# Mask factors copied by GpSimd, earlier turns, other PSUM banks and split last stores in an attention and Fourier-mixing kernel

## The chip, the cores and the metric

The kernel runs on one core of a Trainium2 chip. The metric is the time of one execution on the device, in microseconds (us), as the median of several runs. Besides it there is one profiled execution, whose span, from the first to the last instruction, is about 1 us shorter than the time of a run.

The core has five engines that the text names: TensorE (PE in the profile, its weight loads PEld) multiplies matrices into PSUM; VectorE (DVE), ScalarE (ACT) and GpSimd (POOL) work element by element; SyncE (SP) issues DMA transfers. They run side by side and wait for each other by semaphores. SBUF is the memory on the chip, HBM the one beside it.

## What is computed

Attention with a block mask over 4 batches of 8 heads, then a Fourier mixing and a two-layer network over each batch, all in float32:

```python
# bigbird attention: q, k, v are (4, 8, 768, 64), blocks of 32
scores = q @ k.T / sqrt(64)
# kept: neighbouring blocks, first and last block row and column, 3 sampled blocks a row
attn = softmax(where(mask, scores, -1e9)) @ v
x = attn.transpose(0, 2, 1, 3).reshape(4, 768, 512)
# fnet mixing: w_ch1 is (512, 2048), w_ch2 is (2048, 512)
u = x + real(fft(fft(x, axis=1), axis=2))
un = (u - mean(u)) / sqrt(var(u) + 1e-6)
out = u + maximum(un @ w_ch1, 0) @ w_ch2
```

## The kernel before

The program handles heads two at a time: a *pair* is two heads of one batch, numbered 0 to 15, four for each batch. A pair has 12 *units*: two halves of the queries (384 each), each against six chunks of 128 keys. A *slot* is two units, so a pair has 6 slots. *Phase* p is the four pairs of batch p; from phase 1 on, the mixing and the network of the batch before run beside the attention. Which instruction comes next on each engine is settled while the program is built, by a model of the engines' times (`when`, `busy`, `gap`).

The mask comes in two ways. Where it is made by TensorE, two bfloat16 factors are multiplied into the scores' PSUM bank, which adds a large negative number to the masked ones. The factors lie in buffers that later hold sums (`acc`), so near the end of phase 0 they are copied elsewhere, into a buffer (`big2`) that has held a chunk of the network's weights:

```python
def keep_factors():                                   # called in slot 19 of 24 of phase 0
    kept = room(2, [P, 2, S], "factors", BF16)        # the buffer "big2"
    for a, t in enumerate(factors["at"]):             # at_k and at_q, 128 x 768 each
        nc.sync.dma_start(out=kept[:, a, :], in_=t)
    factors["at"] = kept[:, 0, :], kept[:, 1, :]
...
def w_round(i):            # one of 32 chunks: rounds the weights, ScalarE and then VectorE
    ...
    nc.vector.tensor_add(out=dst, in0=dst, in1=a.bitcast(FP32))      # L462
...
def scores(us):            # for two units
    ...
    nc.tensor.matmul(s[:, i, 0:HS], kT[rows, c * P:(c + 1) * P], qT[rows, queries], ...)      # L570
    ...
    nc.tensor.matmul(s[:, i, 0:HS], at_k[rows, ...], at_q[rows, queries], ...)                # L580
def weigh(u, s):           # exponentials, one of four buffers "e"
    nc.scalar.activation(out=e, in_=s[:, :, 0:HS], func=ACT.Exp, scale=scale)                 # L590
def gather(u):             # sums the six e of a half into "acc", from pair 4 on
    ...
    nc.vector.tensor_tensor(out=acc, in0=start, in1=e, op=ALU.add)                            # L614
    # or, where the model has VectorE busy:
    for i in range(2):
        nc.gpsimd.tensor_add(out=acc[:, i, :], in0=start[:, i, :], in1=e[:, i, :])            # L619
def values(u):             # products of e with v                                             # L633
def total(n):              # row sums of a pair from its two acc, by TensorE                  # L715
```

From pair 5 on, q and k come into the kernel's layout (*turns*) not by TensorE but by these three steps for each pair:

```python
def squares(n, a):         # ScalarE, only for a check on the largest score                   # L527
def flip_blocks(n, a):     # VectorE transposes blocks of 32 x 32: q in place, k into kT
    nc.vector.transpose(out=out, in_=t)                                                       # L537
def in_order(n):           # ScalarE copies q into qT                                         # L545
```

The mixing folds x into sums and differences (VectorE, `fold_0` to `fold_2`, L766 to L794), multiplies along the sequence (`along`, four steps g) and across it (`across`). PSUM has two banks "m", one bank "t" and others. The step g = 2 uses two:

```python
ps = ps_m.tile([P, 512], FP32, tag="m", name="zp")
...
if g == 2:
    side = ps_m.tile([P, 512], FP32, tag="m", name="side")
    at = bank("m")
    ...
...
nc.scalar.copy(out=zs[:, g - 2, 0:KS - 1], in_=ps[:, 0:KS - 1])                               # L845
...
def un_flip(half, m):      # transposes the normalized rows by TensorE
    tag, pool = (("t", ps_t), ("m", ps_m))[half]
def channels(r, half, m):  # products of the network, bank "m"                                # L1089
```

The order within a slot, cut to what matters here:

```python
def slot(sl):
    ...                                  # values of an earlier slot, scores
    for u, ps in got:
        weigh(u, ps)
    if not paired and not late:
        gap(1.5)                         # steps of the mixing, here the folds
    ...
    if BY_VECTOR <= n + 1 < len(pairs):  # turns of the next pair
        for at, fn, args in ((0, squares, (n + 1, 0)), (1, flip_blocks, (n + 1, 0)),
                             (2, in_order, (n + 1,)), (4, flip_blocks, (n + 1, 1)),
                             (5, squares, (n + 1, 1))):
            if s == at:
                fn(*args)
```

The last batch's network uses a scheme with seven block products for each of three output tiles m, and stores two tiles of 128 rows for each m (xA: tile m, xB: tile m + 3). Tile 5, the last of xB, is one transfer of two runs of 64 rows; tile 2, the last of xA, is two transfers of 64 rows.

```python
# outputs(r, m, after): a0, a1 and b0, b1 are the left and right halves of xA and xB
...
plus(b1, p5)
ahead(2)                                               # operands of the next m
plus(b0, product(ps_s, "s", a22, rights[4]))           # sixth product
if r == 1:
    store(1, m)                                        # xB
ahead(3)
p3 = product(ps_m, "m", o_s[m, 4], block(r, 1, 1))     # seventh product
plus(a1, p3)
if r == 1:
    store(0, m)                                        # xA
ahead(4)
```

Of the kernel before, what the change touches and what calls it, by code (L numbers as in the profile page):

```python
# [102 lines left out]
def kernel(  # L103
# [14 lines left out]
    nc = tc.nc  # L118
# [77 lines left out]
    def bank(tag):  # L196

        at = free[tag].index(min(free[tag]))
        when["PE"] = max(when["PE"], free[tag][at])
        free[tag][at] = float("inf")  # L200
        return tag, at
# [273 lines left out]
    def keep_factors():  # L475

        kept = room(2, [P, 2, S], "factors", BF16)
        for a, t in enumerate(factors["at"]):
            nc.sync.dma_start(out=kept[:, a, :], in_=t)
        factors["at"] = kept[:, 0, :], kept[:, 1, :]  # L480

    turned, e_of, acc_of, o_of, sums_of, x_of, sp_of = {}, {}, {}, {}, {}, {}, {}
# [272 lines left out]
    def fourier(b, xA, xB, uns):  # L755
# [45 lines left out]
        def along(g):  # L801

            sa, sd, e1 = st["f"]
            if g == 0:
                st["zc"] = zc_p.tile([P, 2, KS], FP32, tag="zc", name="zc")
            ps = ps_m.tile([P, 512], FP32, tag="m", name="zp")
            odd = S // 4

            def cosine(ps, rows, cols):
                mm = nc.tensor.matmul
                for t in (0, 2):
                    mm(ps[rows, 0:KS], sa[:, t, cols], cs_sb[:, t, :], start=(t == 0), stop=False)  # L814
                mm(ps[rows, 0:odd], e1[:, cols], cs_sb[:, 1, 0:odd], start=False, stop=False)
                mm(ps[rows, odd:KS], sa[:, 1, cols], cs_sb[:, 1, odd:KS], start=False, stop=True)

            def keep_cosine(dst, ps):
                nc.scalar.copy(out=dst, in_=ps[:, 0:KS])

                nc.scalar.copy(out=_grid(dst, P + 1, 2, 63, 63, 1),
                               in_=_grid(ps, P, 2, 65, 63, 1))
                nc.scalar.copy(out=_run(dst, P, 2, P - 1), in_=_run(ps, P + 64, 2, -1))

            if g < 2:
                cosine(ps, slice(0, P), parts[g])
                keep_cosine(st["zc"][:, g, :], ps)
                return
            if g == 2:
                side = ps_m.tile([P, 512], FP32, tag="m", name="side")  # L830
                at = bank("m")
                for i, (lhs, t, cols) in enumerate(((sa[:, 0, :], 0, slice(0, KS)),
                                                    (sa[:, 2, :], 2, slice(0, KS)),
                                                    (e1, 1, slice(0, odd)),
                                                    (sa[:, 1, :], 1, slice(odd, KS)))):
                    g32 = 32 * min(i, 2)
                    nc.tensor.matmul(side[g32:g32 + 32, cols], lhs[:, QD:QD + 32],
                                     cs_sb[:, t, cols], start=True, stop=True,
                                     tile_position=(0, g32))
                st["zs"] = room(0, [P, 3, KS], "zs")  # L840
            zs = st["zs"]
            for t in range(T):
                nc.tensor.matmul(ps[:, 0:KS - 1], sd[:, t, parts[g - 2]], sn_sb[:, t, :],  # L843
                                 start=(t == 0), stop=(t == T - 1))
            nc.scalar.copy(out=zs[:, g - 2, 0:KS - 1], in_=ps[:, 0:KS - 1])  # L845
            if g == 2:
                keep_cosine(zs[0:96, 2, :], side[0:96, :])
                give(at, busy("PE", 0.8) + 1.5)
# [72 lines left out]
        def d(us, fn, *args):  # L921
# [4 lines left out]

        first = [d(1.8, fold_0, 0), d(1.8, fold_0, 1), d(1.0, fold_1, 0), d(0.9, fold_e),
                 d(1.0, fold_1, 1), d(1.2, fold_2, 0), d(0.6, fold_2, 2), d(1.3, fold_2, 1)]
        first += [("M" if g == 2 else "m", lambda g=g: along(g), 2.1, (1.0 if g < 2 else 0.5), 0.0)
                  for g in range(4)]  # L930
        pq = [("m", lambda m=m: across(m), 2.6 if m == 1 else 1.6, 0.7, 0.95) for m in range(T)]
        ar = [[d(1.4 if m == 1 and half == 1 else 1.0, arrive, half, m) for m in range(T)]
# [11 lines left out]
    def mixer(b, xA, xB):  # L944
# [6 lines left out]
        def un_flip(half, m):  # L951
            if half not in unT:
                unT[half] = tr_p.tile([P, ND, T * P], FP32, tag="tr", name="unT")
            un = uns.pop((half, m))
            tag, pool = (("t", ps_t), ("m", ps_m))[half]
            tp = pool.tile([P, ND, P], FP32, tag=tag, name="utp")
            for d in range(ND):
                nc.tensor.transpose(tp[:, d, :], un[:, d * P:(d + 1) * P], ident)  # L958
            nc.scalar.copy(out=unT[half][:, :, m * P:(m + 1) * P], in_=tp)
# [134 lines left out]
            if r == NF // 4 - 1:  # L1094
                store(half, m)

        def store(half, m):
            x = (xA, xB)[half]
            for p0, cnt, rows in _rows(out[b], T * half + m):
                nc.sync.dma_start(out=rows, in_=x[p0:p0 + cnt, m, :])  # L1100
            if m == T - 1:
                finished.add((b, half))

# [34 lines left out]
        def outputs(r, m, after):  # L1138

            if m == 0:  # L1140
                output_left(m, 1)
                output_left(m, 2)
            a11, a12, a21, a22 = (hs[g, i][:, :, m * P:(m + 1) * P]
                                  for i in range(2) for g in range(2))
            a0, a1 = xA[:, m, 0:DH], xA[:, m, DH:DM]
            b0, b1 = xB[:, m, 0:DH], xB[:, m, DH:DM]
            rights = {j: [o_t[j, 0], o_t[j, 1]] for j in (1, 2, 3, 4)}

            def product(pool, tag, a, c):
                ps = pool.tile([P, 512], FP32, tag=tag, name="yy")[:, 0:DH]  # L1150
                for k in range(4):
                    nc.tensor.matmul(ps, a[:, k, :],  # L1152
                                     c[k // 2][:, k % 2, :] if isinstance(c, list) else c[:, k, :],
                                     start=(k == 0), stop=(k == 3))
                busy("PE", 1.75)
                return ps

            def plus(to, a, c=None):
                tt(out=to, in0=a, in1=to if c is None else c, op=ALU.add)
                busy("DVE", 0.43)  # L1160

            def ahead(j):
                if after is not None:
                    output_left(after, j)

            u = sum_p.tile([P, DH], FP32, tag="oT", name="u")
            p1 = product(ps_m, "m", a11, block(r, 0, 0))
            nc.scalar.copy(out=u, in_=p1)
            plus(a0, p1)
            plus(a0, product(ps_m, "m", a12, block(r, 1, 0)))  # L1170
            if m == 0:
                output_left(m, 3)
                output_left(m, 4)
            plus(u, product(ps_t, "t", a21, rights[2]), u)
            plus(a1, u)
            p5 = product(ps_o, "o", o_s[m, 1], rights[1])
            plus(a1, p5)
            ahead(1)
            plus(u, product(ps_s, "s", o_s[m, 3], rights[3]), u)
            both = xB[:, m, :].rearrange("p (n d) -> p n d", n=2)  # L1180
            tt(out=both, in0=both,
               in1=u.rearrange("p (o d) -> p o d", o=1).broadcast_to([P, 2, DH]), op=ALU.add)
            busy("DVE", 0.7)
            plus(b1, p5)
            ahead(2)
            plus(b0, product(ps_s, "s", a22, rights[4]))
            if r == 1:
                store(1, m)
            ahead(3)
            p3 = product(ps_m, "m", o_s[m, 4], block(r, 1, 1))  # L1190
            plus(a1, p3)
            if r == 1:
                store(0, m)
            ahead(4)

        fl = [[("tm"[h], lambda h=h, m=m: un_flip(h, m), 0.6, 0.55, 0.0) for m in range(T)]
              for h in range(2)]

        before = first + [pq[0], ar[0][0], ar[1][0], sp[0][0],
# [44 lines left out]
    def do_apart():  # L1244
# [5 lines left out]
            return  # L1250
        done = state["ready"]
        if kind != "-":
            at = bank(kind.lower())
            done = busy("PE", pe, done) + HOP
        fn()
        if act:
# [7 lines left out]
    def gap(rest=0.0, ahead=None, kinds="tm"):  # L1264
# [4 lines left out]
        while apart:  # L1269
# [7 lines left out]
                if max(when["DVE"], state["ready"]) + dve > when["PE"] + rest + ahead:  # L1277
                    break
            elif kind != "-":
                bank_at = (max if kind == "M" else min)(free[kind.lower()])  # L1280
                if kind.lower() in used or max(state["ready"], bank_at) > when["PE"] + 0.1:
                    break
                used += kind.lower()
            do_apart()
        for item in list(short):
            kind, ready, fn = item
# [48 lines left out]
    def slot(sl):  # L1335
# [25 lines left out]
            sum_up()  # L1361
        for u, ps in got:
            weigh(u, ps)
        if not paired and not late:
            gap(1.5)
        while due and (opens or not paired):
# [70 lines left out]
        while short and (not more or soon) and (  # L1437
# [4 lines left out]
            item = ready[0] if ready else short[0]  # L1442
            short.remove(item)
            item[2]()
        if BY_VECTOR <= n + 1 < len(pairs):
            for at, fn, args in ((0, squares, (n + 1, 0)), (1, flip_blocks, (n + 1, 0)),
                                 (2, in_order, (n + 1,)), (4, flip_blocks, (n + 1, 1)),
                                 (5, squares, (n + 1, 1))):
                if s == at:
                    fn(*args)  # L1450
        w_loads()
        w_steps(sl)
        if sl == SB - 5:
# [143 lines left out]
```

## Time and profile before

| | us |
|---|---|
| time, median of 3 runs (1080.32 to 1081.24) | 1080.54 |
| span of the profiled execution | 1079.5 |
| TensorE busy | 1042.1 (97%) |
| VectorE busy | 661.5 (61%) |
| ScalarE busy | 376.4 (35%) |
| GpSimd busy | 227.4 (21%) |
| mean granted TensorE clock | 0.991 |

A line of a timeline gives the start in us from the start of the span, the duration, the engine, the line of the program (L570 is line 570), the operation, and what it writes and reads; "x6" means six like it in a row. A line of waits gives who waited, for whom, how long in all, how often, and the longest. "Clock" is the share of its full speed that TensorE was granted. A busy engine is one with an instruction in flight; TensorE's instructions overlap, so the sum of theirs is more than the time they took.

### The profile page before, as it was taken

What the parts mean: (1) busy time and instruction counts of PE and PEld (TensorE: products, weight loads), DVE (VectorE), ACT (ScalarE), POOL (GpSimd) and SP (SyncE); (2) the same over time, 40 slices, a digit from 0 to 9 for tenths busy, and PEclk for the clock granted to TensorE, in tenths of its full rate; (3) what the DMA queues carried; (4) which work ended last, traced back from release to release, by engine and by line L of the source; (5) the groups of instructions that cost most, each with busy time, mean ns of one, the idle gap of its engine ahead of it and who ended that gap; (6) DMA issues with size and microseconds to landing.
All of it is one profiled execution on the core that took longest, in us unless ns stands there. A gap on an engine that the chain in (4) does not pass through costs nothing.

```text
span 1079.5 us, 12378 instructions
## 1 busy us (share of the span) xinstructions
PE 1042.1 (97%) x4378; PEld 537.1 (50%) x4378; DVE 661.5 (61%) x1226; ACT 376.4 (35%) x742; POOL 227.4 (21%) x256
## 2 busy tenths in 40 slices
PE   8999789999999999999999999999999999999996
PEld 4433234444455545444444555444444555568575
DVE  5899494777763634764568446665557255675663
ACT  5998555564311202443451302343320212210210
POOL 1000062323600001265454000354630001000000
PEclk9999899999999999999999999999999999999998
DMA  7757222221000001222211000212000001000001
GB/s 224 220 177 239 69 45 44 45 45 30 15 0 1 1 0 30 59 39 42 52 29 31 1 0 18 64 29 39 14 9 7 0 1 30 29 1 1 1 19 43
DMA packets 120769, 47.04 MB, mean 44 GB/s; under 512 B 108142, under 2 KB 113532, under 8 KB 120700
## 3 DMA queue, kind: packets, MB, share of 16 engines
q1 hardware_dynamic: 118812, 45.38, 17.1%
q10 hardware_dynamic: 1856, 0.79, 0.3%
q8 instruction: 36, 0.59, 0.2%
q14 instruction: 33, 0.27, 0.1%
q0 software_dynamic: 32, 0.01, 0.0%
HBM read 37.11 MB, written 6.29 MB: 40 GB/s over the span
## 4 chain that ended last, share of the span: by engine, by line
PE 90%; DVE 6%; issue 2%; ACT 1%; DMA 0%; POOL 0%; SPq 0%; ACTq 0%; POOLq 0%; DVEq 0%
PE y L1089 23%; PE z L1033 15%; PE s L570 12%; PE o L633 11%; PE yp L1033 8%; PE yy L1152 6%; PE xp L1033 4%; PE zp L843 2%; PE sp L701 1%; PE s L580 1%; PE zp L814 1%; PE tp L503 1%; PE utp L958 1%; PE sp L715 1%; PE xt L657 1%
## 5 line engine op out<-in xcount | busy, mean ns | idle before, releaser
L619 POOL TENSOR_TENSOR acc<-acc,e 128x384 f32<-128x384 f32 x154 | 156.8, 1055 | 212.2 <-ACT e L590 137.6
L570 PE MATMUL s<-qT,kT 64*128 64x384 f32 x768 | 154.3, 517 | 7.7 <-DVE kT L537 4.5
L633 PE MATMUL o<-e,vr 128*64 128x384 f32 x768 | 142.8, 500 | 0.0
L1092 DVE TENSOR_TENSOR x<-y,x 128x512 f32<-128x512 f32 x72 | 49.7, 690 | 133.1 <-PE y L1089 133.0
L1089 PE MATMUL y<-w_sb,hA 128*128 128x512 f32 x288 | 129.3, 596 | 1.7 <-ACT zs L845 1.7
L1089 PE MATMUL y<-w_sb,hB 128*128 128x512 f32 x288 | 128.5, 596 | 1.0 <-DVE x L1092 1.0
L595 DVE TENSOR_TENSOR e<-s,mask 128x768 f32<-128x768 f32 x98 | 89.0, 950 | 54.2 <-ACT s L593 48.5
L570 PEld LDWEIGHTS s<-qT,kT 64*128 64x128 f32 x768 | 64.6, 187 | 82.8 <-issue 26.1
L593 ACT ACTIVATE s<-s 128x768 f32<-128x768 f32 x98 | 74.3, 791 | 84.2 <-PE s L570 83.9
L1033 PE MATMUL z<-unT,t 128*128 128x384 f32 x256 | 93.2, 487 | 0.3 <-DVE hA L1038 0.3
L1089 PEld LDWEIGHTS y<-w_sb,hB 128*128 128x128 f32 x288 | 53.4, 190 | 67.7 <-issue 65.3
L590 ACT ACTIVATE e<-s 128x768 f32<-128x768 f32 x94 | 71.2, 812 | 42.6 <-PE s L580 38.6
L1089 PEld LDWEIGHTS y<-w_sb,hA 128*128 128x128 f32 x288 | 53.0, 190 | 65.5 <-issue 58.8
L906 POOL TENSOR_SCALAR st<-st 128x1 f32<-128x1 f32 x24 | 8.3, 348 | 358.8 <-DVE st L905 358.8
L633 PEld LDWEIGHTS o<-e,vr 128*64 128x64 f32 x768 | 48.3, 137 | 71.0 <-issue 67.6
L1038 DVE TENSOR_TENSOR hA<-z,hA 128x384 f32<-128x384 f32 x64 | 35.7, 557 | 77.8 <-PE z L1033 77.8
L1042 ACT ACTIVATE hA<-hA 128x384 f32<-128x384 f32 x64 | 33.4, 523 | 120.4 <-DVE hA L1038 120.3
L619 POOL TENSOR_TENSOR acc<-e 128x384 f32<-128x384 f32 x40 | 42.9, 1094 | 111.9 <-PE sp L715 85.7
L1033 PEld LDWEIGHTS z<-unT,t 128*128 128x128 f32 x256 | 48.5, 190 | 34.7 <-DVE hA L1038 1.3
L1042 ACT ACTIVATE hB<-hB 128x384 f32<-128x384 f32 x64 | 33.5, 523 | 85.9 <-DVE hB L1038 85.9
L1053 ACT COPY hA<-xp 128x384 f32<-128x384 f32 x32 | 15.3, 479 | 113.0 <-PE xp L1033 113.0
L1033 PE MATMUL xp<-unT,w_sb 128*128 128x384 f32 x128 | 47.6, 494 | 2.6 <-DVE x L1092 2.6
(204 smaller groups left out, 1430.8 us busy)
## 6 DMA issues: line engine op xcount, KB each, us to landing
wraw<-in_moe_w_ch_dram SPq DMA_DIRECT2D x32, 512.0 KB
vr<-in_v_dram SPq DMA_DIRECT2D x30, 192.0 KB
qb<-in_q_dram SPq DMA_DIRECT2D x44, 96.0 KB
kb<-in_k_dram SPq DMA_DIRECT2D x44, 96.0 KB
x<-oT SPq DMA_DIRECT2D x192, 12.0 KB
out_dram<-x SPq DMA_DIRECT2D x16, 128.0 KB
out_dram<-x SPq DMA_DIRECT2D x8, 256.0 KB
qr<-in_q_dram SPq DMA_DIRECT2D x24, 64.0 KB
```

Of the source, the lines that this page charges most:

```text
L570: nc.tensor.matmul(s[:, i, 0:HS], kT[rows, c * P:(c + 1) * P], qT[rows, queries], start=True, stop=u not in by_pe)
L590: nc.scalar.activation(out=e, in_=s[:, :, 0:HS], func=ACT.Exp, scale=scale)
L593: nc.scalar.activation(out=s[:, :, 0:HS], in_=s[:, :, 0:HS], func=ACT.Exp, scale=scale)
L595: nc.vector.tensor_tensor(out=e, in0=s[:, :, 0:HS], in1=m.broadcast_to([P, 2, HS]), op=ALU.mult)
L619: nc.gpsimd.tensor_add(out=acc[:, i, :], in0=start[:, i, :], in1=e[:, i, :])
L633: nc.tensor.matmul(o[D * i:D * i + D, :], vt[:, i, c, :], e[:, i, :], start=(c == 0), stop=(c == C - 1))
L1033: nc.tensor.matmul(to, a[:, k, :], c[:, k, :], start=(k == 0), stop=(k == ND // 2 - 1))
L1038: tt(out=to, in0=ps, in1=a, op=ALU.add)
L1042: nc.scalar.activation(out=h, in_=h, func=ACT.Relu)
L1089: nc.tensor.matmul(y, hs[0, half][:, l, m * P:(m + 1) * P], w2_sb[:, 4 * r + l, :], start=(l == 0), stop=(l == 3))
L1092: nc.vector.tensor_tensor(out=x[:, m, :], in0=y, in1=x[:, m, :], op=ALU.add)
L1152: nc.tensor.matmul(ps, a[:, k, :], c[k // 2][:, k % 2, :] if isinstance(c, list) else c[:, k, :], start=(k == 0), stop=(k == 3))
```

## The change

Four things change; all results stay what they were.

1. `keep_factors` copies the two factors by GpSimd and not by two DMA transfers.
2. The turns of the next pair (`squares`, `flip_blocks`, `in_order`) are put right behind the exponentials of the slot, ahead of the mixing steps that `gap` puts in, and no more at the slot's end. They are needed at the next pair's start, while the mixing has more time.
3. The step g = 2 of `along` takes one bank "m" and the bank "t" instead of both banks "m", so that an "m" bank is left for the steps next to it; and `un_flip` of the second half takes the bank "t" for its tile m = 1. The planner is changed to match.
4. In `outputs` the seventh product comes ahead of the sixth, so that xA's tile is stored before xB's; and of the very last tile, the right half of the columns is stored as soon as it is complete, the left half at the end.

```diff
         for a, t in enumerate(factors["at"]):
-            nc.sync.dma_start(out=kept[:, a, :], in_=t)
+            nc.gpsimd.tensor_copy(out=kept[:, a, :], in_=t)
...
             if g == 2:
-                side = ps_m.tile([P, 512], FP32, tag="m", name="side")
-                at = bank("m")
+                side, at = ps_t.tile([P, 512], FP32, tag="t", name="side"), bank("t")
...
-            tag, pool = (("t", ps_t), ("m", ps_m))[half]
+            tag, pool = (("t", ps_t), ("m", ps_m))[half == 1 and m != 1]
...
-        def store(half, m):
+        def store(half, m, cols=slice(0, DM)):
             x = (xA, xB)[half]
-            for p0, cnt, rows in _rows(out[b], T * half + m):
-                nc.sync.dma_start(out=rows, in_=x[p0:p0 + cnt, m, :])
+            for p0, cnt, rows in _rows(out[b][:, cols], T * half + m):
+                nc.sync.dma_start(out=rows, in_=x[p0:p0 + cnt, m, cols])
...
             plus(b1, p5)
+            ends = r == 1 and after is None
+            if ends:
+                store(1, m, slice(DH, DM))
             ahead(2)
-            plus(b0, product(ps_s, "s", a22, rights[4]))
-            if r == 1:
-                store(1, m)
-            ahead(3)
             p3 = product(ps_m, "m", o_s[m, 4], block(r, 1, 1))
             plus(a1, p3)
             if r == 1:
                 store(0, m)
+            ahead(3)
             ahead(4)
 
+            plus(b0, product(ps_s, "s", a22, rights[4]))
+            if r == 1:
+                store(1, m, slice(0, DH if ends else DM))
...
         for u, ps in got:
             weigh(u, ps)
+        if BY_VECTOR <= n + 1 < len(pairs):
+            for at, fn, args in ((0, squares, (n + 1, 0)), (1, flip_blocks, (n + 1, 0)),
+                                 (2, in_order, (n + 1,)), (4, flip_blocks, (n + 1, 1)),
+                                 (5, squares, (n + 1, 1))):
+                if s == at:
+                    fn(*args)
         if not paired and not late:
             gap(1.5)
...
-        if BY_VECTOR <= n + 1 < len(pairs):
-            ...                                        # the same lines, at the slot's end
```

Left out are the lines of the planner, which let a step ask for a bank of each of two kinds ("mt") instead of two of one kind ("M").

More of the change, by code (lines that the diff above doesn't have):

```diff
@@ L928, in fourier @@
                  d(1.0, fold_1, 1), d(1.2, fold_2, 0), d(0.6, fold_2, 2), d(1.3, fold_2, 1)]
-        first += [("M" if g == 2 else "m", lambda g=g: along(g), 2.1, (1.0 if g < 2 else 0.5), 0.0)
+        first += [("mt" if g == 2 else "m", lambda g=g: along(g), 2.1, (1.0 if g < 2 else 0.5), 0.0)
                   for g in range(4)]
@@ L1193, in outputs @@
                 store(0, m)
+            ahead(3)
             ahead(4)
-        fl = [[("tm"[h], lambda h=h, m=m: un_flip(h, m), 0.6, 0.55, 0.0) for m in range(T)]
+            plus(b0, product(ps_s, "s", a22, rights[4]))
+            if r == 1:
+                store(1, m, slice(0, DH if ends else DM))
+        fl = [[("tm"[h == 1 and m != 1], lambda h=h, m=m: un_flip(h, m), 0.6, 0.55, 0.0)
+               for m in range(T)]
               for h in range(2)]
@@ L1252, in do_apart @@
         if kind != "-":
-            at = bank(kind.lower())
+            at = bank(kind[0])
             done = busy("PE", pe, done) + HOP
@@ L1279, in gap @@
             elif kind != "-":
-                bank_at = (max if kind == "M" else min)(free[kind.lower()])
-                if kind.lower() in used or max(state["ready"], bank_at) > when["PE"] + 0.1:
+                bank_at = max(min(free[k]) for k in kind)
+                if (any(k in used for k in kind) or
+                        max(state["ready"], bank_at) > when["PE"] + 0.1):
                     break
-                used += kind.lower()
+                used += kind
             do_apart()
@@ L1444, in slot @@
             item[2]()
-        if BY_VECTOR <= n + 1 < len(pairs):
[L1446 to L1450, printed above, removed]
         w_loads()
```

## The prediction

> **What bounds the kernel now.** I read, in this order: the page's totals, the list of what TensorE waited for, the busy times of chosen stretches, then the timelines of single engines around each hole. The totals and the waits first:
>
> ```profile
> PE 1042.1 (97%) x4378; PEld 537.1 (50%) x4378; DVE 661.5 (61%) x1226; ACT 376.4 (35%) x742; POOL 227.4 (21%) x256
> ...
> PE s L580 <- DMA factors<-at_q: 9.2, 1, 9.2
> PE s L570 <- DVE kT L537: 4.5, 1, 4.5
> PE warm L306 <- POOL ident masks.py:199: 2.6, 1, 2.6
> PE xp L1033 <- DVE x L1092: 2.6, 3, 1.8
> PE y L1089 <- ACT zs L845: 1.7, 3, 0.6
> ```
>
> TensorE is busy 1042 of 1079.5 us, so only about 37 us can be won without taking work from it, and the change takes none: both kernels have the same instructions on it, in another order. Two waits, 9.2 and 4.5 us, are single events; nearly all the rest is 2.6 us at the start and about 9.5 us after its last product. So the change is worth what it does to four holes.
>
> The two big holes cost more than their length. Stretches cut at the events (columns: us of the stretch, then busy us and count of PE, PEld, DVE, ACT and POOL, TensorE clock, DMA share, GB/s):
>
> ```profile
> 106.48:110.92 4.44, 0.00 (x0) 0.00 (x0) 4.21 (x12) 0.68 (x2) 0.00 (x0) 1.00 0.48 140
> 110.92:115.64 4.72, 0.00 (x0) 0.10 (x1) 0.00 (x0) 0.00 (x0) 0.00 (x0) 0.50 0.61 220
> 115.64:121.16 5.52, 5.52 (x22) 1.39 (x21) 0.00 (x0) 1.51 (x2) 0.00 (x0) 0.50 0.00 0
> 121.16:124.60 3.44, 3.44 (x25) 1.51 (x28) 0.77 (x2) 3.28 (x9) 0.00 (x0) 1.00 0.24 40
> 157.82:162.12 4.30, 0.00 (x0) 0.00 (x0) 4.30 (x4) 0.03 (x1) 4.30 (x3) 1.00 0.00 0
> 162.12:165.53 3.41, 3.18 (x12) 1.66 (x12) 3.37 (x6) 0.94 (x2) 1.61 (x2) 0.50 0.38 62
> ```
>
> After each hole the clock stands at 0.50 although TensorE works again: 5.52 us of work at half speed after the first (2.8 us lost) and 3.18 us after the second (1.6 us lost). The holes therefore cost 9.2 + 2.8 = 11.9 us and 4.5 + 1.6 = 6.1 us. Now what VectorE, GpSimd and the queue did around them:
>
> ```profile
> 110.17 0.69 DVE L462 TENSOR_TENSOR w_sb<-w_sb,wraw 128x512 f32<-128x512 f32 x1
> 123.79 0.43 DVE L454 TENSOR_SCALAR wraw<-wraw 128x512 uint32<-128x512 uint32 x1 [12.94 <-ACT wraw L453]
> ...
> 152.42 1.76 DVE L614 TENSOR_TENSOR acc<-acc,e 128x768 f32<-128x768 f32 x1
> 154.10 2.54 DVE L766 TENSOR_TENSOR sa<-x 128x1536 f32<-128x1536 f32 x1
> 156.57 2.55 DVE L766 TENSOR_TENSOR sd<-x 128x1536 f32<-128x1536 f32 x1
> 159.05 1.74 DVE L770 TENSOR_TENSOR sa<-sa 128x765 f32<-128x765 f32 x1
> 160.71 1.49 DVE L537 STREAM_TRANSPOSE kT<-kb 128x768 f32<-128x768 f32 x1
> ...
> 166.66 0.95 DVE L614 TENSOR_TENSOR acc<-acc,e 128x768 f32<-128x768 f32 x1
> ```
>
> ```profile
> 142.49 6.24 POOL L619 TENSOR_TENSOR acc<-acc,e 128x384 f32<-128x384 f32 x6 [137.41 <-ACT e L590]
> 153.56 10.18 POOL L619 TENSOR_TENSOR acc<-acc,e 128x384 f32<-128x384 f32 x6 [0.20 <-ACT e L590]
> ...
> 110.92 0.53 SPq L479 DMA_DIRECT2D factors<-at_k  x1
> 111.50 0.60 SPq L479 DMA_DIRECT2D factors<-at_q  x1
> ```
>
> The reader sees that the copy of the factors was issued at 110.92, 0.06 us after VectorE's last step (110.17 + 0.69 = 110.86) on the weight chunk whose buffer it takes. So 4.4 us of the first hole is VectorE's lag, and only 4.7 us the transfer's. In the second hole the turn of kT stands behind three folds of the mixing.
>
> **What the Trainium skill says.** "TensorE: Matmul & The Clock Gate", Part 1, says that the clock is halved after an idle window of some 3.4 us and restored after a busy one, on a free-running grid. The trace agrees: half clock began 4.44 and 4.30 us into the holes and lasted 10.24 and 3.41 us, three windows and one. "GPSIMD Engine Reference", section 3.1, gives 1.03 to 1.8 cycles an element at 1.2 GHz for work with one input; no such copy is in this trace. "SBUF — State Buffer", "Who interferes with whom", says that VectorE instructions with two SBUF inputs contend with GpSimd's reads: six adds took 6.24 us beside little VectorE work and 10.18 us beside the folds, 1.04 against 1.70 us each. "DMA: Bandwidth & Descriptors", rules for kernel authors, says that the slowest dimension above 1 caps the number of DMA engines; tile 5 is stored as two runs of 64 rows, so two engines. The trace's DMA share agrees, below.
>
> **Part 1, GpSimd copies the factors.** It must wait for the same buffer, 110.86. By the skill's figures 768 elements take 768 x 1.03 to 1.8 / 1.2 GHz = 0.66 to 1.15 us (estimate); I take 1.0 us for each of the two, as VectorE is idle there. TensorE starts at about 113.0 and not 115.64: 2.6 us. The clock grid has edges at 110.92, 114.33, 117.75 and 121.16. The window to 114.33 is idle for over half, the next one is full, so the clock should return at 117.75: 4.75 us at half speed, 2.4 us lost instead of 2.8. Sum: 3.0 us.
>
> **Part 2, turns right behind the exponentials.** The turn of kT now stands before the folds, at about 154.2 to 155.7, and TensorE, which is ready at 157.8, doesn't wait for it. That would be the whole 6.1 us. But the folds move by the same 1.5 us, VectorE's sum of work up to the L614 at 166.66 is the same, and that gather gets no earlier. Following the new order by hand, with 1.9 us for two units' scores with their mask and 1.45 us for their products with the values, as in TensorE's timeline: scores of pair 5 from 157.8 to 159.75; products with the values to 161.2; scores to 163.1; products to 164.6. Next in TensorE's order come the row sums of pair 4 (L715), which need this gather: 166.66 + 0.95 = 167.6. So TensorE waits again, about 3.0 us from 164.6. That is under one clock window, so no half clock. The kernel before passed the same point, the next scores, at 171.2; the new one at 167.65 + 0.8 for the row sums = 168.4. Gain 2.8 us, where 6.1 was to be had.
>
> **Part 3, other banks.** The mixing step g = 2 took both "m" banks, so the channel product behind it waited for ScalarE's copy of zs: 1.7 us in three times. With its side tile in the "t" bank the next product uses the free "m" bank. I count 1.5 us. The bank of one un_flip in six I count as nothing: TensorE shows no wait of that kind over 0.3 us.
>
> **Part 4, the last stores.** The end of the run: queue issues, then stretches (columns as above):
>
> ```profile
> 1068.80 0.56 SPq L1100 DMA_DIRECT2D out_dram<-x  x1
> 1070.52 1.55 SPq L1100 DMA_DIRECT2D out_dram<-x  x2
> ...
> 1072.00:1075.00 3.00, 0.00 (x0) 0.00 (x0) 0.00 (x0) 0.00 (x0) 0.00 (x0) 0.75 0.53 124
> 1075.00:1077.00 2.00, 0.00 (x0) 0.00 (x0) 0.00 (x0) 0.00 (x0) 0.00 (x0) 0.50 0.15 54
> 1077.00:1079.50 2.50, 0.00 (x0) 0.00 (x0) 0.00 (x0) 0.00 (x0) 0.00 (x0) 0.50 0.00 1
> ```
>
> The last product ends at 1070.0. From 1075 to 1077 the DMA share is 0.15, or 2.4 of 16 engines: the two that carry tile 5 (issued 1068.80) still work at 54 GB/s and hold up the last pieces of tile 2 behind it. After the change tile 5 leaves in halves: the first when b1 is complete, which by the last adds is 0.5 us earlier (about 1068.3), the second when b0 is, at 1070.5. Both halves use the same two engines and the bytes are the same 128 KB on each, so it is a start 0.5 us earlier and one issue less at the end (0.5 us), against pieces of 1 KB. I count 0.9 us.
>
> **Sum.** 3.0 + 2.8 + 1.5 + 0.9 = 8.2 us; 1080.5 - 8.2 = 1072.3 us.
>
> **Rivals.** (a) No new wait: the gather doesn't stand in the way, and part 2 gives its 6.1 us; time 1069. For it: the planner also reshares gathers between VectorE and GpSimd (VectorE has two fewer that open an accumulator). Against it: the order still has this gather behind the folds. (b) The new wait is worse: GpSimd, at 1.7 us an add beside the folds, falls behind, buffers for e come free late, the exponentials stop, and TensorE idles a whole window and runs at half clock; part 2 gives nothing, time 1075. For it: only four e buffers, and 10.18 us for three units where TensorE needs 3.3 us for two. (c) The 1 KB pieces cost as much time as those of 2 KB: the tail grows by 2 to 3 us, time about 1075. (d) The copies cost 2 us each, as a GpSimd add of 768 elements would (2 x 1055 ns): part 1 gives 0.5 to 1 us, time 1074.5. (e) The new order brings small waits in later stages, such as the 1.8 us at one xp; 1 or 2 us either way.
>
> **Range and chances.** Parts 1 and 2 are each uncertain by 2 us up and 3 down, the tail by 1 to 2, the later stages by 1.5. Together some 4 us either way: 1068.5 to 1076.5. Two per cent would need a gain of 21.6 us, more than all four holes leave, or a loss that nothing points to: within 2% has 0.98, faster 0.01, slower 0.01.
>
> **What would show it right or wrong.** Part 1: two GpSimd copies starting with the end of VectorE's L462, 1 us each, and TensorE idle for 6.5 us before L580. Part 2: no wait for kT, and instead one of about 3 us at L715 for VectorE's gather, with no half clock after it. Part 3: no waits of TensorE for zs. Part 4: 8.5 us from the last product to the end, not 9.45. Wrong it would be if the clock stayed halved, if the wait moved to exponentials that wait for GpSimd, or if stretches after 200 us, where TensorE now idles for 8 us in all, gained a new hole.

## The result and the profile after

The changed kernel took 1078.2 us (median; single runs from 1076.9 to 1079.2) where the kernel before took 1080.4 us beside it. The ratio is 0.9978, with a 95% interval from 0.9961 to 0.9996: a gain of 2.4 us, between 0.4 and 4.2. Predicted were 8.2 us and a time of 1072.3 us, with a range that began at 1068.5 and ended at 1076.5. The profiled executions differ by more than the medians, 1079.5 against 1075.5 us of span: the one before took 1081.2 us, 0.8 over its median, the one after 1077.3, 0.9 under its own (so the spans are 1.7 to 1.8 us shorter than the times). About 1 us of the difference is where the free-running clock grid happened to lie at the start: TensorE first got its full clock at 6.11 us after the change and at 8.52 before it, and the first scores came 1 us earlier.

The page's totals first, which hardly moved:

```profile
PE 1041.3 (97%) x4378; PEld 535.8 (50%) x4378; DVE 666.0 (62%) x1226; ACT 375.8 (35%) x742; POOL 231.1 (21%) x258
```

Now what TensorE waited for (engine and line, for whom; us in all, times, the longest):

```profile
PE s L580 <- POOL factors L479: 6.2, 1, 6.2
PE sp L715 <- DVE acc L614: 3.8, 1, 3.8
...
PE xt L657 <- ACT unT L958: 2.0, 1, 2.0
```

The wait for the factors is down from 9.2 to 6.2 us. The 4.5 us for kT are gone, but two waits are new, and one was not predicted: the row sums wait 3.8 us for a gather, and the transposes L657 wait 2.0 us for a copy of ScalarE. The three waits for `zs` (1.7 us in all) are gone.

Stretches cut at the two big holes (us of the stretch, then busy us and count of PE, PEld, DVE, ACT and POOL, TensorE clock, DMA share, GB/s):

```profile
105.41:109.93 4.52, 0.00 (x1) 0.00 (x0) 4.22 (x12) 0.69 (x2) 0.00 (x0) 0.84 0.46 142
109.93:111.58 1.65, 0.00 (x0) 0.10 (x1) 0.00 (x0) 0.00 (x0) 1.59 (x2) 0.50 0.87 270
111.58:115.34 3.76, 3.76 (x16) 1.10 (x19) 0.00 (x0) 1.51 (x2) 0.00 (x0) 0.50 0.11 45
...
161.01:164.85 3.84, 0.00 (x0) 0.00 (x1) 3.77 (x6) 0.00 (x0) 2.27 (x2) 0.78 0.00 0
164.85:169.95 5.10, 5.10 (x17) 1.86 (x18) 4.19 (x7) 1.11 (x2) 0.00 (x0) 0.50 0.01 3
```

The first hole is 6.17 us and 3.76 us of work at half clock follow, where 9.16 and 5.52 were before. The second hole is 3.84 us long, and behind it TensorE works 5.10 us at half clock, which costs another 2.55 us. Before, 3.18 us of work were at half clock there. So the second place costs as much as it did: 6.4 us against 6.1.

The first hole and the copies of GpSimd, in the timeline:

```profile
109.93 0.82 POOL L479 COPY factors<-at_k 128x768 bf16<-128x768 bf16 x1 [104.82 <-DVE w_sb L462]
110.70 0.83 POOL L479 COPY factors<-at_q 128x768 bf16<-128x768 bf16 x1
```

They start with the end of VectorE's L462, as foreseen, and take 0.8 us each. The second hole:

```profile
161.18 2.27 POOL L619 TENSOR_TENSOR acc<-e 128x384 f32<-128x384 f32 x2 [1.72 <-ACT e L590]
161.37 1.23 DVE L788 TENSOR_TENSOR sa<-sa 128x384 f32<-128x384 f32 x1
162.53 1.07 DVE L787 TENSOR_TENSOR e<-e 128x128 f32<-128x128 f32 x1
...
163.84 0.95 DVE L614 TENSOR_TENSOR acc<-acc,e 128x768 f32<-128x768 f32 x1
```

While TensorE waits for the gather L614, VectorE still has folds in front of it, and two of these are stretched: beside GpSimd's adds they take 1.23 and 1.07 us, where the same two took 0.56 (384 elements) and 0.29 us (128 elements) in the kernel before, with GpSimd idle:

```profile
165.65 0.56 DVE L788 TENSOR_TENSOR sa<-sa 128x384 f32<-128x384 f32 x1
166.13 0.29 DVE L787 TENSOR_TENSOR e<-e 128x128 f32<-128x128 f32 x1
```

That is 1.4 us. The row sums themselves are cut in two by the wait (first the kernel before, then the changed one):

```profile
170.42 0.85 PE L715 MATMUL sp<-acc,pick 128*32 128x384 f32 x8
...
160.17 0.84 PE L715 MATMUL sp<-acc,pick 128*32 128x384 f32 x4
164.85 1.50 PE L715 MATMUL sp<-acc,pick 128*32 128x384 f32 x4 [3.85 <-DVE acc L614]
```

Eight matmuls took 0.85 us together. Now four take 0.84 us ahead of the wait, and the other four 1.50 us at half clock behind it, so the cut costs some 0.7 us besides the wait and the clock. The third place, around 230 us:

```profile
229.49 1.88 ACT L545 COPY qT<-qb 128x256 f32<-128x256 f32 x6
231.27 0.58 ACT L958 COPY unT<-utp 128x512 f32<-128x512 f32 x1
231.91 0.55 PE L657 MATMUL xt<-ident,oT 128*128 128x128 f32 x3 [1.99 <-ACT unT L958]
```

The six copies of `in_order` now stand ahead of the copy of `unT` on ScalarE. That copy empties the bank "t", which `xt` needs, and TensorE waits 1.99 us for it. At the very end:

```profile
1066.00:1069.00 3.00, 0.00 (x0) 0.00 (x0) 0.03 (x1) 0.00 (x0) 0.00 (x0) 0.78 0.49 120
...
1070.00:1073.00 3.00, 0.00 (x0) 0.00 (x0) 0.00 (x0) 0.00 (x0) 0.00 (x0) 0.50 0.15 47
```

The last product ends at 1065.57, the span at 1075.50: a tail of 9.93 us, not the predicted 8.5, and longer than the 9.44 before. A DMA share of 0.15 is still 2.4 engines of 16.

### The profile page after: what moved, and what is told of

Its sections match the earlier page's. It is cut to its first block, busy times and chain, and to the rows that moved or that the text cites. A ratio compares the mean times of both kernels' runs of the same rounds, so it can differ in the third digit from the quotient of the medians.

```text
span 1075.5 us, 12390 instructions
## 1 busy us (share of the span) xinstructions
PE 1041.3 (97%) x4378; PEld 535.8 (50%) x4378; DVE 666.0 (62%) x1226; ACT 375.8 (35%) x742; POOL 231.1 (21%) x258
## 4 chain that ended last, share of the span: by engine, by line
PE 87%; DVE 7%; ACT 2%; DMA 1%; issue 1%; POOL 1%; SPq 1%; DVEq 0%; ACTq 0%; POOLq 0%
PE y L1088 22%; PE z L1032 15%; PE s L570 11%; PE o L633 10%; PE yp L1032 7%; PE yy L1151 6%; PE xp L1032 4%; PE zp L842 2%; PE s L580 1%; PE sp L701 1%; DMA wraw<-in_moe_w_ch_dram 1%; PE zp L814 1%; PE utp L957 1%; DVE x L743 1%; PE sp L715 1%
## 5 line engine op out<-in xcount | busy, mean ns | idle before, releaser
L619 POOL TENSOR_TENSOR acc<-acc,e 128x384 f32<-128x384 f32 x150 | 152.3, 1054 | 85.2 <-DVE e L595 83.1
L590 ACT ACTIVATE e<-s 128x768 f32<-128x768 f32 x94 | 71.6, 813 | 47.2 <-PE s L580 33.6
L619 POOL TENSOR_TENSOR acc<-e 128x384 f32<-128x384 f32 x44 | 48.0, 1110 | 126.6 <-PE sp L715 93.5
L1032 PE MATMUL z<-t,w_sb 128*128 128x384 f32 x128 | 46.7, 488 | 1.0 <-DVE t L994 1.0
```

The lines of the kernel that those rows point to most:

```text
L1032: nc.tensor.matmul(to, a[:, k, :], c[:, k, :], start=(k == 0), stop=(k == ND // 2 - 1))
```

## The experiments

In words, the theory after reading this: the copies and the banks give what they promised or more; the early turns lose, because the folds still stand in front of a gather that TensorE needs, and because of ScalarE's copies; the halves of the last tile share two DMA engines and bring nothing. The rivals: the turns do help, and something else takes the gain (the banks, or the planner's other order); the tail sets the difference; or all of it is the clock. Differences in us below are the measured ratio times 1080.5.

**GpSimd's copies alone**, on the kernel before:

```diff
-            nc.sync.dma_start(out=kept[:, a, :], in_=t)
+            nc.gpsimd.tensor_copy(out=kept[:, a, :], in_=t)
```

> The kernel before with the GpSimd copies alone. Theory (the turns' gain was handed on to a new wait, the copies gave what they were to give): two copies of 0.8 us, the hole before L580 6.2 us and not 9.2, half clock for two windows and not three: 3 to 4 us faster, about 1077. Rival (the gain that is there comes from elsewhere, and a shorter hole only moves the wait to VectorE's lag): 0 to 1 us.

Measured: ratio 0.9972 [0.9963, 0.9982], a gain of 3.0 us. The wait for the factors is 6.2 us as in the changed kernel. The part is worth what was predicted.

**The early turns alone**, on the kernel before: the six lines of the turns move from the slot's end to right behind `weigh`.

> The kernel before with the turns put right behind the exponentials, nothing else. Theory: the 4.5 us wait for kT is gone, a wait of 3 to 4 us at the row sums L715 for VectorE's gather L614 is there instead, with half clock behind it, and another one of up to 2 us near 230 us behind ScalarE's six copies of q: between 1 us faster and 2.5 us slower. Rival (the turns win their 6 us, and the banks or the stores lose them): 5 to 6 us faster.

Measured: ratio 1.0043 [1.0029, 1.0056], a loss of 4.6 us. TensorE's waits show the same two new lines, here without any other part of the change:

```profile
PE sp L715 <- DVE acc L614: 3.8, 1, 3.8
...
PE xt L657 <- ACT unT L959: 2.0, 1, 2.0
```

So both waits come from the turns. Behind the first, 5.15 us of work ran at half clock. The two profiled spans differ by 2.7 us, but the one with the turns had its first scores 1.0 us earlier (8.24 against 9.28), by the clock grid at the start; without that it is 3.7 us. The medians of the runs differ by 3.7 us too (1084.6 and 1080.9); one run of the five, of 1087.7 us, is far above the others.

**Both bank changes alone**, on the kernel before:

```diff
-                side = ps_m.tile([P, 512], FP32, tag="m", name="side")
-                at = bank("m")
+                side, at = ps_t.tile([P, 512], FP32, tag="t", name="side"), bank("t")
...
-            tag, pool = (("t", ps_t), ("m", ps_m))[half]
+            tag, pool = (("t", ps_t), ("m", ps_m))[half == 1 and m != 1]
```

> The kernel before with the other banks alone. Theory: the three waits of 0.57 us for zs are gone: 1.5 us faster, give or take 1 for other small waits. Rival (the bank t is now contended): 1 to 3 us slower.

Measured: ratio 0.9968 [0.9956, 0.9980], a gain of 3.5 us, more than twice the predicted 1.5.

**The side tile's bank alone**, without that of `un_flip`:

> The kernel before with the side tile of step g = 2 in the bank t, and un_flip's bank as it was. Theory (the side tile alone frees the bank that the products waited for): 3 to 4 us faster, as with both. Rival (un_flip's bank brings what the prediction did not count): 1.5 to 2 us faster.

Measured: ratio 0.9959 [0.9946, 0.9973], a gain of 4.4 us. The intervals of the two overlap, so the bank of `un_flip` adds nothing that can be measured. TensorE's waits of the later stages, of this kernel:

```profile
PE y L1088 <- DVE x L1091: 1.4, 4, 0.3
PE xp L1032 <- DVE x L1091: 1.1, 3, 0.4
```

No line for `zs` is left, and the three waits at `xp` fell from 2.6 to 1.1 us, the longest from 1.8 to 0.4. Those at `y` for VectorE rose from 1.0 to 1.4.

**The new order and the halves of the last stores alone**, on the kernel before:

> The kernel before with the new order and the halves of the last stores alone. Theory: the two DMA engines that carry the last tile set the end as before, now with two starts: from the last product to the end 9.9 us and not 9.45, 0.5 us slower. Rival, as predicted: 0.9 us faster.

Measured: ratio 1.0006 [0.9999, 1.0013], a loss of 0.6 us that can't be told from none. The profiled tail is 11.1 us against 9.4, but this execution was the slowest of the 21 (1083.7 us). In the changed kernel and the three below that keep its stores it is 9.9 to 10.0 us.

**The changed kernel without the early turns** (their lines back at the slot's end):

> The changed kernel without the earlier turns: copies, banks and stores only. Theory (the earlier turns lose 2 to 4 us, the other parts together win 5 to 6): the wait at L715 and the one at 232 us are gone, the wait for kT is back; 1074 to 1075.5, so 3 us faster than the changed kernel. Rival (the turns only lose alone, and pay once the copies are there): about 1078 or slower.

Measured: ratio 0.9948 [0.9935, 0.9962], a gain of 5.6 us on the kernel before, 3.2 us more than the whole change. The sum of the single parts is a gain of 3.0 - 4.6 + 3.5 - 0.6 = 1.3 us, and together they measured 2.4 (0.4 to 4.2): the parts about add up.

**Other order of the folds.** In the changed kernel, the folds of the differences `sd` of the first mixed batch come after the first two steps of `along`, which need only `sa`. Then two of the big folds stand behind the gather and not in front of it. Nothing is left out.

```diff
+        if b == 0:
+            first = [first[i] for i in (0, 2, 3, 5, 6, 8, 9, 1, 4, 7, 10, 11)]
```

> The changed kernel, in which for the first batch the folds of sd come behind the first two steps along the sequence, so that VectorE reaches the last gather of pair 4 some 3.5 us earlier. Theory (the row sums L715 wait for the gather behind the folds): the 3.85 us wait at L715 falls under 1 us, no half clock follows it, 4 to 6 us faster than the changed kernel, about 1073. Rival (GpSimd's slow adds hold the gather, not the folds): the wait stays over 2.5 us, and the time within 1.5 us of the changed kernel.

Measured: ratio 0.9924 [0.9911, 0.9938], a gain of 8.2 us on the kernel before and 5.8 on the changed one. L715 waits 0.16 us, and the clock stays whole where 5.10 us ran at half speed:

```profile
160.00:170.00 10.00, 9.84 (x56) 4.53 (x56) 8.76 (x9) 4.04 (x10) 7.18 (x6) 1.00 0.02 5
```

It was the folds that held up the gather. This run alone doesn't rule out GpSimd's share of the sums, as the planner shifted that too: ahead of the row sums GpSimd makes four adds of L619 here in 6.63 us and not six in 10.26, and VectorE one gather more. But in the changed kernel those six adds were done at 159.46, before TensorE ran out of work at 161.01, and VectorE went without a pause from fold to fold until the gather began at 163.84.

**The last store over 16 engines.** In the changed kernel, a0's product with a12 comes sixth and not second, for every m; xB is stored ahead of xA, and xA, whose last tile is two transfers of 64 rows, comes last.

```diff
-            plus(a0, product(ps_m, "m", a12, block(r, 1, 0)))            # was second
...
+            plus(b0, product(ps_s, "s", a22, rights[4]))
+            if r == 1:
+                store(1, m, slice(0, DH if ends else DM))
+            plus(a0, product(ps_m, "m", a12, block(r, 1, 0)))
             p3 = product(ps_m, "m", o_s[m, 4], block(r, 1, 1))
...
-            plus(b0, product(ps_s, "s", a22, rights[4]))                 # was last
-            if r == 1:
-                store(1, m, slice(0, DH if ends else DM))
```

> The changed kernel, in which the product for a0 comes sixth and not second, so that the last tile of xB is complete and stored two products before the end, and xA's last tile, which 16 DMA engines share, is stored last. Theory (the two engines that carry the last tile of xB set the end): from the last product to the end about 7.5 us and not 9.9, 2 us faster than the changed kernel. Rival (the end is the fixed time of any last transfer): 9.5 to 10 us as before, no faster.

Measured: ratio 0.9983 [0.9976, 0.9989], a gain of 1.8 us on the kernel before, no more than the changed kernel. But the tail is 6.92 us and not 9.93:

```profile
1072.00:1074.00 2.00, 0.00 (x0) 0.00 (x0) 0.00 (x0) 0.00 (x0) 0.00 (x0) 0.63 0.67 171
```

Once the last product has ended, the transfers take a share of 0.67 at 171 GB/s, and there are no two engines left over that go on for 3 us. What the tail won was lost again in the middle: with the later product, TensorE waits 1.9 and 1.5 us for VectorE's operands of the tile m = 0 (L1151 for L1134).

**The old factors for longer.** In the changed kernel the copies are made as before, but the scores of phase 0 go on reading the old factors; the copies are used from slot 24 on.

```diff
-        factors["at"] = kept[:, 0, :], kept[:, 1, :]
+        factors["next"] = kept[:, 0, :], kept[:, 1, :]
...
     # at the start of a slot
+        if sl == SB:                                   # 24
+            factors["at"] = factors["next"]
```

> The changed kernel, in which the scores read the factors in their old place up to the end of phase 0 and in the new one only from phase 1 on, so that TensorE doesn't wait for the copies. Theory (most of the hole left before L580 is VectorE's lag, 4.4 us, which the copies wait for): the hole of 6.2 us and its half clock, 1.9 us, are gone; 5 to 8 us faster than the changed kernel, 1070 to 1073. Rival (VectorE's lag is only put off and comes back as a longer wait at L715): 0 to 2 us faster.

Measured: ratio 0.9903 [0.9890, 0.9917], a gain of 10.5 us on the kernel before and 8.1 on the changed one. The whole first hole is gone, and its half clock too:

```profile
100.00:112.00 12.00, 12.00 (x89) 4.74 (x83) 10.53 (x23) 9.79 (x25) 1.59 (x2) 1.00 0.73 221
```

TensorE works all 12 us at full clock while GpSimd copies (1.59 us). VectorE's lag of 4.5 us on the weight chunk, which made most of the hole, is still there, but nobody waits for it, here or later.

**All repairs together**: the folds' order, the old factors, and the new order of the last products, now only for the very last tile (`if ends:`), so that the others keep theirs.

> The changed kernel with the three repairs: factors read in their old place up to phase 1, folds of sd later, and for the very last output tile alone the product for a0 sixth. If the three causes are separate, their gains add up: 8.9 + 5.8 from the earlier runs and 2.5 to 3 at the end: about 1061. If the lag of VectorE was only covered by the hole before L580, it comes back at L715 or at kT: 1065 or slower.

Measured: ratio 0.9811 [0.9798, 0.9824], a gain of 20.4 us. The single repairs give 5.8 + 8.1 and, from the tail (7.1 us in this kernel's profile), 9.9 - 7.1 = 2.8 us on top of the change's 2.4: 19.1. One wait of 1.71 us, at L657 for ScalarE's copy of `unT`, is left, and with it a half clock:

```profile
215.97:219.39 3.42, 1.71 (x13) 0.88 (x11) 3.28 (x6) 2.65 (x9) 1.55 (x2) 1.00 0.03 7
219.39:222.80 3.41, 3.41 (x13) 1.43 (x14) 0.74 (x2) 0.81 (x2) 0.00 (x0) 0.50 0.72 116
```

The window of the clock from 215.97 was busy for half; the next one was halved, which cost as much again as the wait. This execution was the slowest of the five (1062.9 us against 1060.2 to 1060.9, with a mean clock of 0.997 against 0.998 to 0.999), so the half clock is probably missing from the others.

**The same repairs without the early turns:**

> The same three repairs without the earlier turns. Theory (the turns are worth something once the gather isn't behind the folds, as the wait for kT is 4.5 us and its half clock 1.6): 3 us or more slower than with them. Rival (with the folds of sd moved, the old place of the turns is early enough): the same or, without the copies of q ahead of the bank's release, 2 us faster.

Measured: ratio 0.9852 [0.9837, 0.9867], a gain of 16.0 us. So beside the repairs the early turns are worth 20.4 - 16.0 = 4.4 us; without them TensorE waits 3.4 and 0.6 us for kT. (The profile puts the 3.4 us down to the fold L787, which came last; but these scores read kT, whose turn ended at 149.22, and began at 149.37. In the kernel before, the scores followed the turn by the same 0.15 us.)

**The same repairs, with ScalarE's copies of q late**: the transposes of VectorE stay early, `in_order` goes back to the slot's end.

```diff
-                                 (2, in_order, (n + 1,)), (4, flip_blocks, (n + 1, 1)),
-                                 (5, squares, (n + 1, 1))):
+                                 (4, flip_blocks, (n + 1, 1)), (5, squares, (n + 1, 1))):
...
     # at the slot's end
+        if s == 2 and BY_VECTOR <= n + 1 < len(pairs):
+            in_order(n + 1)
```

> The same three repairs with the block transposes and the squares early, and only ScalarE's six copies of q back at the end of the slot. Theory (these copies, 1.9 us, in front of unT's copy make the 2.0 us wait of xt at L657): that wait is gone, 1.5 to 2 us faster than with all turns early. Rival: the wait stays, the same time.

Measured: 1060.0 us (1059.0 to 1060.2), ratio 0.9804 [0.9791, 0.9818], a gain of 21.2 us. The wait for `unT` is gone, and no work in the middle of the profile ran at half clock. This version beats both kernels, and with the same computation. Against the version with all turns early the time isn't distinguishable (1060.0 and 1060.5, intervals that overlap), so the expected 1.5 to 2 us did not show. Part of it went into a wait at L715, 0.8 us where it was 0.2.

## Why the prediction was wrong, point by point

**Part 1, right.** Predicted 3.0 us, measured 3.0. The copies take 0.8 us where the estimate took 1.0; the hole is 6.2 us instead of 6.5, and half clock lasted two windows, as worked out from the grid.

**Part 2, wrong, and with it the whole.** The step that failed is "That is under one clock window, so no half clock. ... Gain 2.8 us, where 6.1 was to be had." The first half of the chain was right: the wait for kT went, and a wait at L715 for VectorE's gather took its place. Four things were not as put there. The wait is 3.8 and not 3.0 us: GpSimd's adds of pair 5 stretch the folds ahead of the gather by 1.4 us, while half of the row sums, 0.8 us, ran ahead of the wait. The row sums, cut in two, cost 0.7 us more. Half clock followed all the same, 2.55 us: the grid's window from 159.71 to 163.13 was 38% busy, so not idle, and the next two were halved. And ScalarE's part of the turns, six copies that the prediction never followed, put 2.0 us of wait in the way at 230 us. In the profile the turns remove 6.1 us and add 3.85 + 2.55 + 0.7 + 2.0 = 9.1, a loss of 3.0. Measured alone they lose 4.6 us (3.1 to 6.1) where a gain of 2.8 was predicted. That 7.4 us is more than the whole distance between prediction and result. The wait and its half clock are shown to be causes by the fold order, which takes both away and gains 5.8 us; the copies of `in_order` by putting them back, after which that wait is gone, though its effect on the time was within the noise. The cut of the row sums is read from the traces alone. Of the loss, 0.7 us (by the medians) to 1.6 us (by the ratio) stays unexplained. Two of the prediction's own signs of being wrong came true: the clock stayed halved, and a new hole opened after 200 us.

The rivals fared so: (a), no new wait, fell. (b), a worse wait that leaves part 2 with nothing, came nearest: half clock and no gain. But GpSimd was not what held TensorE. Exponentials did wait for buffers, 1.4 us for GpSimd's adds and then longest for the same late gather of VectorE:

```profile
164.89 0.81 ACT L590 ACTIVATE e<-s 128x768 f32<-128x768 f32 x1 [4.59 <-DVE acc L614]
```

TensorE waited for that gather itself, at the row sums, and the folds stood in front of it. Of (c), the pieces of 1 KB, about 0.3 us of 2 to 3 is there (part 4); (d), slow copies, fell (part 1). (e), new small waits in later stages, happened once, 2.0 us, at a place that had been put down as a margin.

**Part 3, right in kind, too small.** The term "I count 1.5 us" measured 3.5 and 4.4 us in its two runs. Only the waits for `zs` had been counted. The free bank also let the products L1033 run at better times: their wait fell from 2.6 to 1.1 us. The waits agree in size: in the two profiles TensorE's idle time, span less busy, fell from 37.4 to 34.2 and 33.6 us, of which 0.2 and 0.5 us are a shorter wait for the factors. The bank of `un_flip` adds nothing that can be measured, as predicted.

**Part 4, wrong.** The step that failed is "it is a start 0.5 us earlier and one issue less at the end". Predicted was a gain of 0.9, measured a loss of 0.6 (-0.1 to 1.4). The start did come 0.5 us earlier: the first packet of the last stores started 0.60 us before the last product's end, and 0.04 us before it in the kernel before. But from the first packet to the last it then took 8.2 us (1064.97 to 1073.13) and not 7.1 (1069.99 to 1077.09), and that sets the end, not the number of issues. The prediction took the same bytes on two engines to need the same time. Some 0.3 us of the 1.1 come from the smaller pieces, an estimate from the packet records: within a run, packets of 1 KB start 42 ns apart and those of 2 KB 80 ns, and each of the two engines has 128 of the one instead of 64 of the other. The rest is open. Slow packets, of 0.2 to 0.55 us where others take 0.05 to 0.08, stand where the halves meet the pieces of tile 2: the first half's last packet ends at 1068.32, the second half's first starts at 1069.47, and tile 2's last ends at 1069.90. The Trainium skill, "DMA: Bandwidth & Descriptors", on why a DMA increments its semaphore by 16 (the part "How many engines"), says that a narrow transfer takes the lowest-numbered engines. That fits: the records don't number the engines, but from 1068.4 the packets start in two chains, the pieces of tile 2 first and the second half behind them. The tail fell to 6.9 us when the transfer that comes last was one over 16 engines.

**The sum.** 3.0 - 4.6 + 3.5 - 0.6 = 1.3 us from parts measured alone, 2.4 together, 8.2 predicted. The chance for "within 2%" was right; the range failed, since it gave part 2 only "2 us up and 3 down".

## What to carry to other kernels

An instruction moved forward on an in-order engine moves the ones behind it back: follow every engine that takes part (here VectorE, ScalarE and GpSimd) to the next place where the bound engine waits for it, and move the work that nobody waits for, not only the one that somebody does. Here the fold order and the old factors were worth 5.8 and 8.1 us, more than any part of the change. And before a wait is shortened, ask whether its reader can go on with the old copy; that removed the wait altogether.

## What the runs showed of the hardware

The Trainium skill, "TensorE: Matmul & The Clock Gate", Part 1, speaks of an idle window and a busy one. In these traces the clock changes only on a grid with a step of 3.41 us, and windows of it that were busy in part were enough to halve it: windows that were 38% busy (the changed kernel, at 159.71) and 50% busy (the repaired one, at 215.97) were followed by half clock. The hole of 1.99 us at L657, cut by an edge of the grid, was not; its emptier window was 57% busy in the changed kernel and 54% with the turns alone. But the share alone does not decide. In the kernel before, a window 47% busy, with a hole of 1.82 us inside it, kept the clock whole (columns as above):

```profile
694.60:698.02 3.42, 1.59 (x7) 0.87 (x5) 3.38 (x5) 0.59 (x1) 3.42 (x4) 1.00 0.15 53
698.02:701.43 3.41, 3.41 (x12) 2.06 (x11) 1.94 (x4) 0.48 (x1) 0.45 (x1) 1.00 0.46 139
```

What else counts is not shown. Once halved, the clock came back after windows that were 86, 87, 89 and 93% busy or more, and not after ones of 82% or less. The place of the grid mattered: the same wait of 4.5 us for kT was followed by one window of half clock in the kernel before (162.12 to 165.53) and by two in the one with GpSimd's copies alone (159.00 to 165.82). So a hole under 2 us cost nothing or half a window more, and the skill's figure of a whole idle window is too lenient for a kernel with many short holes. That this is what spreads the changed kernel's runs over 2.3 us (1076.9 to 1079.2) is likely, but only argued.

VectorE's folds were stretched from 0.56 to 1.23 and from 0.29 to 1.07 us beside GpSimd's adds, and in the kernel before six of these adds took 10.18 us beside the folds and 6.24 beside little VectorE work. So each slowed the other.
